# First expert's first unit as plain block products in two halves of 256 tokens, with the first loads issued from two engines

## The chip, the cores and the metric

The kernel runs on one core of a Trainium2 chip, in one launch. The metric is device time in microseconds (us), the median of the runs of a kernel.

## The reference

Two stages follow each other. The first is attention by chunks of 32 tokens (4 batches, 8 heads, 768 tokens, 64 dimensions), where each chunk sees 16 tokens to its left, 8 to its right and 8 memory keys per head:

```python
scores = scale * np.matmul(q_c, k_full.transpose(0, 1, 3, 2))
scores = scores - np.max(scores, axis=-1, keepdims=True)
a = np.exp(scores)
a = a / (np.sum(a, axis=-1, keepdims=True) + 1e-09)
out[:, :, c_start:c_end] = np.matmul(a, v_full)
```

Its output, as x of 3072 tokens by 512, goes through a layer of 8 experts (F = 1024), whose weights P come from exp of the logits by eight rounds of row and column normalisation:

```python
for e in range(E):
    h = np.maximum(x @ w1[e], 0.0)
    ye = h @ w2[e]
    out += P[:, e:e + 1] * ye
```

## The kernel before, in words

**Units.** The experts' work is cut into 48 units, each one expert and a group of 512 tokens (6 groups, 8 experts). A unit has four parts of the hidden dimension (`fp`, 0 to 3; tile names end in it). A unit's hidden products are px, py, pz (L1272), its output products yx, yy, yz or, for expert 0, yp (`plain_output`, L1684). The products have float32 accuracy: every operand is split into two fp16 parts under a power-of-two scale (`split`: the high part on ACT, L462, then the low part on VectorE, L470), and three products of the parts are added (`PASSES`). A group of operands has one scale; `scales` finds it from the largest magnitude: per-partition maxima on VectorE (`vmax` of v for x, L780; `mxs` of the weights, L503), a transposed row through PE (row_x, row_w, L443), the exponent on VectorE, and back to all partitions through PE (sp_x, sp_w, L430), then ux, sx (or uw, sw) at L405 and L406.

**Seven products.** Hidden products use a scheme of seven products over 2 x 2 blocks in place of eight; its operands are the blocks and four sums of blocks, made of x on GpSimd and VectorE (xt, L1019 to L1043) and of w1 on GpSimd (ws, L562, in `cut`), and split too. A unit takes 7 x 24 = 168 matmuls of 256 columns. Expert 0's outputs use w2 as it stands.

**Attention.** 24 blocks of 128 tokens, four to a group of x. For a block: `load_block`, `load_extra` and `load_values` issue its loads (v at L758 and memory values at L748, into a ring of two v tiles), `transposed` turns q and k (tq L817, tk L821, tx L695; copies qT, kC on ACT), `scores` makes sp on PE (L880), the maximum and the subtraction on VectorE (sm, s), exp on ACT (L924), the totals on VectorE, a product on GpSimd (s, L930), and `values` turns s (ta, L953), multiplies by v (xp, L963) and copies to xg. `build` makes the operands of a group of x; it needs all four blocks and their common scale. `logits` makes lp (L1089).

**First weights.** `first_weights` loads w1 and w2 of expert 0 through SP, takes the maxima and the scale, and calls `cut` for sums and splits.

**The order.** A planner in Python (`Plan`) takes tasks with an engine, a cost and a due time, and writes each engine's order by list scheduling. `START`, `TURN`, `UNIT`, `AHEAD` (50, 68, 36.7, 62) set the due times: `begin(n)` for unit n, `needed(n)` for block n of attention. Where it expects PE to be idle, `Plan.pad` puts warm matmuls (tile warm, L376), which compute nothing that is used. DMAs are issued by SP, and 16 by ACT (memory values of the first two blocks); an issue stands in the engine's order, and what comes behind it on that engine waits for it. Both engines' DMAs complete on one set of semaphores.

Of the kernel before, what the change touches and what calls it, by code (L numbers as in the profile page):

```python
# [203 lines left out]
def tile_chunked_attn_sinkhorn_moe(  # L204
# [28 lines left out]
    P = 128  # L233
# [58 lines left out]
    sx = misc.tile([P, NU], F32, name="sx")  # L292
    ux = misc.tile([P, NU], F32, name="ux")
    sw = misc.tile([P, E, 2], F32, name="sw")
    uw = misc.tile([P, E, 2], F32, name="uw")
    most_of = misc.tile([P, 2, NU + 2 * E + 1], F32, name="most_of")
# [12 lines left out]
    START, TURN, UNIT, AHEAD = 50.0, 68.0, 36.7, 62.0  # L309
# [229 lines left out]
    def cut(e, fp, which, st, ld, prio):  # L539
        s = sw[:, e, which - 1 : which]  # L540
        if e == 0 and which == 2:

            o = operands("w2", [P, 2, 7, DH], f"w2_{e}_{fp}")
            wide = "p a d -> p (a d)"
            done = split(
                lambda j: o.t[:, j, 0:4].rearrange(wide),
                lambda: st.t.rearrange(wide),
                s,
                [known[e, 2], ld],
                prio,  # L550
                (1.15, 1.28),
                [st, o],
            )
            wo[e, fp, 2] = (o, [done])
            return
# [31 lines left out]
        o = operands("w1" if which == 1 else "w2", shape, f"w{which}_{e}_{fp}")  # L587
# [14 lines left out]
        else:  # L602
# [9 lines left out]
        done = [split(d, src, s, deps, prio - 2, costs, [st, o]) for d, src, costs in parts]  # L612
        done.append(
            split(
                lambda j: o.t[:, j, 3:7].rearrange(flat),
                lambda: ws.t.rearrange(flat),
                s,
                deps + sums,
                prio,
                (1.15, 1.28),  # L620
                [ws, o],
            )
        )
        wo[e, fp, which] = (o, done)
# [11 lines left out]
    lgs = []  # L636

    BU = UT // QB
# [91 lines left out]
    def load_values(n):  # L730
# [8 lines left out]
        slot = n % 2  # L739
        vt = rings["v"].take(lambda k: v_tiles[k], slot)  # L740

        queue, eng = (nc.scalar, "ACT") if n < 2 else (nc.sync, "SP")

        def go_m():
            for par in range(2):
                p0 = par * KW + WIN
                for c in range(CB):
                    queue.dma_start(  # L748
                        vt.t[p0 : p0 + NM, c], mem_v[b, par::2].rearrange("h m d -> m h d")
                    )  # L750

        def go_v():
            for par in range(2):
                p0 = par * KW

                def part(c, r, t, m):

                    nc.sync.dma_start(  # L758
                        vt.t[p0 + r : p0 + r + m, c],
                        v[b, par::2, t : t + m].rearrange("h t d -> t h d"),  # L760
                    )
# [11 lines left out]
        at = needed(n) - 22.0  # L773
        lv = [add("SP", 2 * CB + 2 * (first or last), go_v, (), at, [vt], dma=2.5)]
# [13 lines left out]
        vfound.append(add("DVE", 1.21, most, lv, needed(n) - 3.0, [vt]))  # L788
        if n % BU == BU - 1:
            u = n // BU  # L790
            sxs[u] = scales(
                lambda: vmax[:, n + 1 - BU : n + 1],
                sx[:, u : u + 1],
                ux[:, u : u + 1],
                f"x_{u}",
                vfound[n + 1 - BU : n + 1],
                needed(n) - 2.0,
                "att",
            )
# [60 lines left out]
    def scores(n):  # L860
# [51 lines left out]
        t = add("PE", 1.5, go, made, at, [qT, kC, s], takes=sp)  # L912
# [72 lines left out]
    def build(u, at):  # L985
# [5 lines left out]

        def plain(i, kt, g, r):
# [12 lines left out]
        def sums(kt):  # L1005
# [53 lines left out]

        for kt in range(2):  # L1060
            plain(0, kt, g1, kt)
            sums(kt)
# [3 lines left out]
        xkept[u] = add(  # L1066
            "SP",
            1,
            lambda: nc.sync.dma_start(xkeep[u], x.t.rearrange("p a o k n -> p (a o k n)")),
            done,  # L1070
            at + 10.0,
            [x],
            dma=7.0,
        )
# [167 lines left out]
    def expert_scale(e, prio):  # L1242
        pscales[e] = add(
            "DVE",
            0.29,
            lambda: nc.vector.tensor_scalar(
# [6 lines left out]
            ),  # L1253
# [36 lines left out]
    def hidden(e, u, fp, hs, use_at, aside):  # L1290
# [5 lines left out]
        def run(dst, op, more, deps, takes=None):  # L1296
# [4 lines left out]
                    (w.t[:, wl, a, kt], x.t[:, xl, b, kt]) for kt in range(2) for wl, xl in PASSES  # L1301
# [365 lines left out]

    def plain_output(n, t, hs):

        e, u = units[n]  # L1670
# [4 lines left out]
        a = buf("acc", apool, [P, DM], F32, f"acc_{e}_{T}")  # L1675
        py = bank("main", [P, DM], f"yp_{e}_{T}")

        def part(fp):
            def go():
                hf, wf = hs[fp][0], wo[e, fp, 2][0]  # L1680
                for i, (fh, (hl, wl)) in enumerate(
# [5 lines left out]
                        wf.t[:, wl, 2 * fh : 2 * fh + 2].rearrange("p a d -> p (a d)"),  # L1687
# [7 lines left out]
        for fp in range(FP):  # L1695
# [4 lines left out]
                [t, *hs[fp][1], *wo[e, fp, 2][1]],  # L1700
                now[0],
                [hs[fp][0], wo[e, fp, 2][0]],
# [24 lines left out]
    def first_weights():  # L1727
        for which, at in ((1, START), (2, outputs_at(0) - 20.0)):
            found, staged = [], []
            for fp in range(FP):  # L1730
# [126 lines left out]
```

## Time and profile before

| What | us |
|---|---|
| median of 3 runs (1969.32 to 1970.98) | 1970.33 |
| the profiled execution | 1967.24 |
| its span | 1965.5 |
| PE busy | 1931.7 |
| VectorE (DVE) busy | 1465.9 |
| ScalarE (ACT) busy | 1031.5 |
| GpSimd (POOL) busy | 557.3 |

The profile is of one execution; the busy times add up rows that may overlap with other engines' work, and what an engine waits for is inferred from semaphores. Times in the tables and timelines count from the start of the span.

### The profile page before, as it was taken

What the parts mean: (1) busy time and instruction counts of PE and PEld (TensorE: products, weight loads), DVE (VectorE), ACT (ScalarE), POOL (GpSimd) and SP (SyncE); (2) the same over time, 40 slices, a digit from 0 to 9 for tenths busy, and PEclk for the clock granted to TensorE, in tenths of its full rate; (3) what the DMA queues carried; (4) which work ended last, traced back from release to release, by engine and by line L of the source; (5) the groups of instructions that cost most, each with busy time, mean ns of one, the idle gap of its engine ahead of it and who ended that gap; (6) DMA issues with size and microseconds to landing.
All of it is one profiled execution on the core that took longest, in us unless ns stands there. A gap on an engine that the chain in (4) does not pass through costs nothing.

```text
span 1965.5 us, 47252 instructions
## 1 busy us (share of the span) xinstructions
PE 1931.7 (98%) x19536; PEld 1665.8 (85%) x19536; DVE 1465.9 (75%) x2406; ACT 1031.5 (52%) x2014; POOL 557.3 (28%) x568
## 2 busy tenths in 40 slices
PE   8899999989999999999999999999999999999998
PEld 7776777768888888888888888888888888888887
DVE  4975655897678885798678886798678886787574
ACT  4655555555565564565455464565455464464353
POOL 2321111254214332342214322332214322232112
PEclk9999999999999999999999999999999999999999
DMA  7785532244413632343423642343423642322321
GB/s 163 177 236 148 134 95 71 103 156 145 143 74 103 218 137 89 111 156 135 137 79 97 220 140 82 118 157 128 141 81 98 208 152 81 108 82 82 124 82 65
DMA packets 242183, 248.45 MB, mean 126 GB/s; under 512 B 114736, under 2 KB 176176, under 8 KB 237616
## 3 DMA queue, kind: packets, MB, share of 16 engines
q1 hardware_dynamic: 241328, 245.31, 39.3%
q8 instruction: 153, 2.51, 0.5%
q14 instruction: 62, 0.51, 0.1%
q10 hardware_dynamic: 640, 0.13, 0.0%
HBM read 184.04 MB, written 61.34 MB: 125 GB/s over the span
## 4 chain that ended last, share of the span: by engine, by line
PE 92%; DVE 6%; DMA 1%; issue 0%; SPq 0%; ACT 0%; POOL 0%; ACTq 0%; DVEq 0%; POOLq 0%
PE px L1272 24%; PE yx L1272 22%; PE pz L1272 12%; PE yz L1272 11%; PE py L1272 6%; PE yy L1272 6%; PE yp L1684 6%; PE xp L963 2%; DVE ss L1428 1%; DVE c L1329 1%; DVE w L470 1%; PE sp L880 1%; DVE x L470 1%; PE ta L953 1%; DVE h L1472 1%; PE warm L376 1%
## 5 line engine op out<-in xcount | busy, mean ns | idle before, releaser
L1272 PEld LDWEIGHTS <-w 128*128 128x128 f16 x8064 | 788.3, 98 | 110.9 <-issue 16.7
L1272 PEld LDWEIGHTS <-h 128*128 128x128 f16 x7056 | 691.1, 98 | 82.7 <-ACT h L1439 1.0
L1272 PE MATMUL px<-x,w 128*128 128x256 f16 x4608 | 563.3, 273 | 12.1 <-DVE c L1329 12.0
L1593 POOL TENSOR_TENSOR acc<-acc,y 128x256 f32<-128x256 f32 x252 | 275.5, 1100 | 886.7 <-ACT y L1568 883.7
L1272 PE MATMUL yx<-w,h 128*128 128x256 f16 x4032 | 469.6, 273 | 1.4 <-ACT h L1439 0.7
L1319 ACT ACTIVATE q<-px 128x256 f32<-128x256 f32 x384 | 145.9, 381 | 317.5 <-PE px L1272 312.9
L1272 PE MATMUL pz<-x,w 128*128 128x256 f16 x2304 | 284.0, 273 | 2.3 <-ACT q L1319 2.3
L1272 PE MATMUL yz<-w,h 128*128 128x256 f16 x2016 | 233.8, 273 | 0.0
L1488 DVE TENSOR_TENSOR h<-ss,h 128x1024 f16<-128x1024 f32 x160 | 205.8, 1298 | 3.5 <-ACT h L1464 3.5
L1439 ACT ACTIVATE h<-c 128x768 f16<-128x768 f32 x168 | 140.8, 838 | 113.2 <-DVE c L1329 113.2
L1464 ACT CAST h<-ss 128x1024 f16<-128x1024 f32 x168 | 174.1, 1039 | 15.7 <-DVE ss L1428 15.7
L1472 DVE SCALAR_TENSOR_TENSOR h<-c,h 128x768 f16<-128x768 f32 x168 | 168.3, 1005 | 11.7 <-ACT h L1439 11.6
L1428 DVE SCALAR_TENSOR_TENSOR ss<-c,ss 128x256 f32<-128x256 f32 x336 | 166.8, 496 | 8.0
L1329 DVE SCALAR_TENSOR_TENSOR c<-px,q 128x256 f32<-128x256 f32 x192 | 78.2, 421 | 115.1 <-PE px L1272 111.3
L1272 PE MATMUL py<-x,w 128*128 128x256 f16 x1152 | 142.5, 273 | 0.0
L1568 ACT ACTIVATE y<-yx,pscale 128x256 f32<-128x256 f32 x168 | 79.3, 473 | 113.1 <-PE yx L1272 109.5
L1428 DVE SCALAR_TENSOR_TENSOR ss<-c,h 128x512 f32<-128x512 f32 x168 | 129.7, 772 | 7.5 <-ACT h L1416 6.3
L1684 PE MATMUL yp<-w,h 128*128 128x512 f16 x576 | 132.0, 379 | 0.0
L1329 DVE SCALAR_TENSOR_TENSOR c<-py,q 128x256 f32<-128x256 f32 x192 | 80.8, 424 | 68.2 <-PE py L1272 59.8
L1272 PE MATMUL yy<-w,h 128*128 128x256 f16 x1008 | 116.9, 273 | 0.0
L1684 PEld LDWEIGHTS <-h 128*128 128x128 f16 x576 | 55.2, 98 | 58.8 <-issue 0.8
L462 ACT ACTIVATE w<-ws,sw 128x1024 f16<-128x1024 f32 x60 | 68.5, 1142 | 64.9 <-POOL ws L562 64.9
(129 smaller groups left out, 1815.0 us busy)
## 6 DMA issues: line engine op xcount, KB each, us to landing
x<-xkeep SPq DMA_DIRECT2D x28, 1792.0 KB
akeep<-acc SPq DMA_DIRECT2D x168, 256.0 KB
acc<-akeep SPq DMA_DIRECT2D x168, 256.0 KB
w1f<-in_moe_w_dram SPq DMA_DIRECT2D x64, 256.0 KB
w2f<-in_moe_w_dram SPq DMA_DIRECT2D x32, 512.0 KB
w1fm<-in_moe_w_dram SPq DMA_DIRECT2D x56, 256.0 KB
w2fm<-in_moe_w_dram SPq DMA_DIRECT2D x28, 512.0 KB
xkeep<-x SPq DMA_DIRECT2D x6, 1792.0 KB
```

What stands on the lines that cost most here:

```text
L462: lambda: nc.scalar.activation(dst(0), src(), AF.Copy, scale=s),
L1272: nc.tensor.matmul(dst.t, a, b, start=(not more and n == 0), stop=(n == end), skip_group_check=more,)
L1319: lambda: nc.scalar.activation(t.t, src.t, AF.Copy, scale=DOWN),
L1329: lambda: nc.vector.scalar_tensor_tensor(c.t[:, o], src.t, DOWN, q.t, op0=ALU.mult, op1=ALU.add),
L1428: lambda: nc.vector.scalar_tensor_tensor(dst(), src(), 0.0, other(), op0=ALU.max, op1=op),
L1439: lambda: nc.scalar.activation(h.t[:, 0, 0:3], c.t, AF.Relu),
L1464: lambda: nc.scalar.copy(h.t[:, 0, 3:7], ss.t),
L1472: lambda: nc.vector.scalar_tensor_tensor(h.t[:, 1, 0:3].rearrange("p a n -> p (a n)"), c.t.rearrange("p a n -> p (a n)"), 0.0, h.t[:, 0, 0 ...
L1488: lambda: spare.tensor_tensor(h.t[:, 1, 3:7], ss.t, h.t[:, 0, 3:7], op=ALU.subtract),
L1568: (lambda: nc.scalar.activation(t.t, src.t, AF.Copy, scale=f))
L1593: lambda: nc.gpsimd.tensor_tensor(acc.t[:, cols], acc.t[:, cols], q.t, op=ALU.add),
L1684: nc.tensor.matmul(py.t, hf.t[:, hl, where[fh], o : o + P], wf.t[:, wl, 2 * fh : 2 * fh + 2].rearrange("p a d -> p (a d)"), start=(fp == 0 ...
```

## The change

The first unit (expert 0, tokens 0 to 511) computes its hidden products as eight plain block products per part, 192 matmuls of 256 columns (tile pp, L1830 of the changed kernel), in two halves of 256 tokens. The first half needs blocks 0 and 1 of attention alone and has a scale of its own (column NU of sx and ux); `expert_scale` corrects `pscale` for its tokens. w1 and w2 of expert 0 are split as they stand, 1024 columns at once. w1 is loaded a second time after that unit, for the sums of the later units, and the other operands of the group of x are made after it (`rest`). v of the first four blocks has four places, two of them in tiles of w2; the split x of block 2 and 3 lies partly in such a tile too. v of these blocks and w1, w2 of expert 0 are issued by SP and ACT in turn; memory values are loaded once per block and parity and copied twice by SP (`copy_m`) in place of eight loads. The planner's numbers change with it.

```diff
-    START, TURN, UNIT, AHEAD = 50.0, 68.0, 36.7, 62.0
+    START, TURN, UNIT, AHEAD = 44.0, 64.0, 36.7, 58.0
+    PACE = 46.0
...
+        if e > 0:
+            pieces = [(slice(3, 7), slice(0, 4), (1.15, 1.28))]
+        else:
+            pieces = [(slice(2, 3), slice(0, 1), (0.5, 0.65)), (slice(4, 7), slice(1, 4), (0.9, 1.1))]
+            deps = deps + o.users
...
+    def plain1(fp, st, ld, prio):
+        o = operands("w1", [P, 2, 7, 2, P], f"w1_0_{fp}")
+        done = split(
+            lambda j: o.t[:, j, 0:4].rearrange("p o k f -> p (o k f)"),
+            lambda: st.t.rearrange("p a k f -> p (a k f)"),
+            sw[:, 0, 0:1],
+            [known[0, 1], ld],
...
         if n < BU:
-            return 12.0 + 9.0 * n
-        return START + ((n + 1) / BU - 1.0) * AHEAD - 12.0
+            return 11.0 + 6.5 * n
+        return PACE + ((n + 1) / BU - 1.0) * AHEAD - 12.0
...
-        slot = n % 2
-        vt = rings["v"].take(lambda k: v_tiles[k], slot)
-        queue, eng = (nc.scalar, "ACT") if n < 2 else (nc.sync, "SP")
+        slot = n if n < BU else n % 2
+        if slot < 2:
+            vt = rings["v"].take(lambda k: v_tiles[k], slot)
+        else:
+            vt = rings["v"].take(
+                lambda k: room(k, 0, WIDE * 2)
...
+        if n < BU:
+            lv = [
+                add(eng, parts, lambda i=i, on=on: go_v((i,), on), (), at, [vt], dma=1.25)
+                for i, (eng, on) in enumerate((("SP", nc.sync), ("ACT", nc.scalar)))
+            ]
+        else:
+            lv = [add("SP", 2 * parts, lambda: go_v((0, 1), nc.sync), (), at, [vt], dma=2.5)]
         if vmem.get(slot) != b:
             vmem[slot] = b
-            lv.append(add(eng, 2 * CB, go_m, (), at + 0.1, [vt], dma=0.4))
+            eng, queue = ("ACT", nc.scalar) if n < BU else ("SP", nc.sync)
+            lv.append(add(eng, 2, go_m, (), at - 0.1, [vt], dma=0.1))
+            lv.append(add("SP", 2, copy_m, [lv[-1]], at + 0.1, [vt], dma=0.3))
...
+            (NU, n == BU // 2 - 1, START - 12.0),
...
-        t = add("PE", 1.5, go, made, at, [qT, kC, s], takes=sp)
+        t = add("PE", 0.9, go, made, at, [qT, kC, s], takes=sp)
...
+        if u == 0:
+            for i, (g, cs, k) in enumerate(
+                ((g1, c1, 0), (g1, c1, 1), (g2, c2, 1), (g2, c2, 0))
+            ):
...
+                v = NU if i < 2 else u
...
+                        cs + [sxs[v]],
...
+            def rest(at):
+                before = list(x.users)
...
+                for kt in range(2):
+                    sums(kt, at, done)
+                keep(at, done)
...
+            if e == 0:
+                nc.vector.tensor_scalar(
+                    pscale[:, 0, 0:TH],
...
+    def first_hidden(fp, g, h):
...
+        for i, fh in enumerate(((0, 1), (1, 0))[g]):
+            px = bank("main", [P, GT], f"pp_{nm}_{fh}")
+            t = None
+            for k in range(2):
+                def go(fh=fh, k=k, px=px):
+                    for n, (kt, (wl, xl)) in enumerate(
+                        (kt, p) for kt in range(2) for p in PASSES
+                    ):
+                        nc.tensor.matmul(
+                            px.t,
+                            w.t[:, wl, 2 * fh + k, kt],
+                            tokens(k, kt, xl),
...
+    def first_unit():
+        hs = [operands("h", [P, 2, 7, GT], f"h_0_{fp}") for fp in range(FP)]
+        for g in range(2):
+            made = [first_hidden(fp, g, hs[fp]) for fp in range(FP)]
+            for t in range(TH):
+                plain_output(0, g * TH + t, made)
...
-    first_weights()
+    def fetch_first(which, at, step):
+        found, staged = [], []
+        for fp in range(FP):
+            st, ld = load(0, fp, which, at - 42.0 + step * fp, eng=("SP", "ACT")[fp % 2])
...
+        if n == 0:
+            for fp, s in enumerate(fetch_first(2, START + 14.0, 2.0)):
+                plain2(fp, *s, START + 8.0 + 2.0 * fp, vs[fp][0].users if fp > 1 else [])
+            first_unit()
+            later[0](needed(BU + 1))
+            for fp in range(FP):
+                weights(0, fp, 1, begin(1) - 10.0 + 2.0 * fp)
+            maxima(1, begin(3))
+            continue
```

The order of PE ahead of the first hidden product, before (tq, tk and sp_1089 are the transposes and scores of block 5, lq a transpose of the logits):

```order
L430 MATMUL sp_x_969<-most_of,one 128x1
...
L817 MATMUL tq_980<-ident,q_680 128x128 x4
...
L1110 MATMUL lq_997<-ident,lt_972 128x128
L821 MATMUL tk_1003<-ident,k_682 128x128 x4
...
L880 MATMUL sp_1089<-kC,qT_989 32x64 x32
...
L1272 MATMUL px_0_0_1129<-x_999,w_0_0_759 128x256
```

The same place in the change (sp_611, ta and xp are of block 2, tk and sp_841 of block 3, tx of the second four blocks, x_657 holds the first half of x):

```order
L952 MATMUL sp_611<-kC,qT_539 32x64 x32
...
L445 MATMUL row_w_0_705<-ident,most_of 1x128
...
L1025 MATMUL ta_715<-ident,s_663 128x128 x4
L432 MATMUL sp_w_0_721<-most_of,one 128x1
...
L893 MATMUL tk_750<-ident,k_414 128x128 x4
L737 MATMUL tx_759<-ident,kx_408 128x128 x4
...
L1830 MATMUL pp_0_0_0_767<-x_657,w_0_0_727 128x256
...
L1035 MATMUL xp_800<-at_723,w_0_2_267 64x32 x32
L952 MATMUL sp_841<-kC,qT_741 32x64 x32
```

The first product moves from behind the scores of block 5 to a place ahead of the values product of block 2. Ahead of the first yp now stand 132 pp (of 192), ahead of the first px before stood the four values products that now lie among them in part; the change has 159 warm matmuls ahead of the first product (195 before) and 4 behind it.

ACT from its start to the first exp, before:

```order
L748 DMA v_144<-in_mem_v_dram 8x4x64 x8
L748 DMA v_145<-in_mem_v_dram 8x4x64 x8
L845 ACT_TABLE_LOAD
L845 ACTIVATE qT_233<-tq_228 128x512
...
L699 COPY kxT_273<-tx_268 128x512
...
L845 ACTIVATE qT_345<-tq_338 128x512
L924 ACTIVATE s_343<-s_343 128x512
```

and in the change:

```order
L796 DMA v_145<-in_mem_v_dram 8x4x64 x2
L815 DMA v_145<-in_v_dram 56x4x64 x4
L917 ACT_TABLE_LOAD
L917 ACTIVATE qT_213<-tq_208 128x512
L496 DMA w1f_1_228<-in_moe_w_dram 128x4x128 x2
...
L496 DMA w1f_3_241<-in_moe_w_dram 128x4x128 x2
L796 DMA w_0_2_267<-in_mem_v_dram 8x4x64 x2
...
L815 DMA w_0_2_267<-in_v_dram 56x4x64 x4
...
L815 DMA w_0_3_346<-in_v_dram 56x4x64 x4
L996 ACTIVATE s_349<-s_349 128x512
```

Ahead of the table load stand 13 issues (16 before); 16 more stand between the copies of block 0, the last ten behind kxT, and the first exp and block 1's qT come behind them.

VectorE ahead of the first output product, in the change (behind the second half of x):

```order
L472 SCALAR_TENSOR_TENSOR x_657<-xt_0_1169,sx,x_657 128x4x256
L407 TENSOR_SCALAR uw<-sp_w_0_1382 128x1
L408 RECIPROCAL sw<-uw 128x1
L963 MEMSET sp_1303 32x2x4x16
L966 TENSOR_REDUCE sm_1405<-sp_1303 128x2x4
L972 TENSOR_TENSOR s_1420<-sp_1303,sm_1405 128x2x4x64
L472 SCALAR_TENSOR_TENSOR w_0_0_1174<-w2f_0_764,sw,w_0_0_1174 128x1024
```

The first yp stands behind that last split, as before; ahead of it now stand also the low parts of four hidden tiles (512 columns each), sums of x and two splits of them, which before lay ahead of the first hidden product.

## Rows read from the trace of the kernel before

**Rows 1.** The page: its first line, section 1 and the chain by engine

```profile
span 1965.5 us, 47252 instructions
...
PE 1931.7 (98%) x19536; PEld 1665.8 (85%) x19536; DVE 1465.9 (75%) x2406; ACT 1031.5 (52%) x2014; POOL 557.3 (28%) x568
...
PE 92%; DVE 6%; DMA 1%; issue 0%; SPq 0%; ACT 0%; POOL 0%; ACTq 0%; DVEq 0%; POOLq 0%
```

**Rows 2.** PE by stretches: stretch, length, busy (instructions), granted clock, DMA share, GB/s

```profile
50.00:63.29 13.29, 8.52 (x138) 0.99 0.71 139
...
63.29:80.00 16.71, 16.71 (x187) 0.90 0.89 265
```

**Rows 3.** The same table for the warm tile alone, on PE

```profile
0.00:63.29 63.29, 27.52 (x195) 0.94 0.74 159
...
92.53:352.00 259.47, 2.46 (x18) 1.00 0.53 142
```

**Rows 4.** Timeline of PE, 0 to 64 us: start, duration, instruction, idle before

```profile
16.82 1.09 PE L817 MATMUL tq<-ident,q 128*128 128x128 f32 x4 [3.38 <-DMA q<-in_q_dram]
...
21.68 1.04 PE L880 MATMUL sp<-kC,qT 64*32 64x64 f32 x64
...
29.09 2.06 PE L963 MATMUL xp<-at,v 64*64 64x32 f32 x64
...
38.36 0.27 PE L443 MATMUL row_w<-ident,most_of 128*1 128x128 f32 x1
...
62.45 0.91 PE L880 MATMUL sp<-kC,qT 64*32 64x64 f32 x64 [4.37 <-DVE s L900]
...
63.29 2.74 PE L1272 MATMUL px<-x,w 128*128 128x256 f16 x12
```

**Rows 5.** Timeline of PE behind the first product

```profile
72.63 1.47 PE L1272 MATMUL px<-x,w 128*128 128x256 f16 x12
...
73.94 1.47 PE L1272 MATMUL pz<-x,w 128*128 128x256 f16 x12
...
92.53 5.34 PE L1684 MATMUL yp<-w,h 128*128 128x512 f16 x24
```

**Rows 6.** Timeline of ACT, its first entry (q: issuing of DMAs)

```profile
0.72 7.20 ACTq L748 DMA_DIRECT2D v<-in_mem_v_dram  x16
```

**Rows 7.** Tile w1f and tile v, 0 to 50 us, the issuing rows of SP

```profile
L494 SPq DMA_DIRECT2D w1f<-in_moe_w_dram x8: 497/511/1985, 19.7 to 29.1; - x8
...
L758 SPq DMA_DIRECT2D v<-in_v_dram x34: 288/412/1842, 7.4 to 44.6; - x34
```

**Rows 8.** All engines by stretches of 5 us: the columns of Rows 2, every engine's busy time

```profile
15.00:20.00 5.00, 3.18 (x15) 2.76 (x16) 2.17 (x4) 1.25 (x3) 0.00 (x0) 0.53 0.50 108
...
20.00:25.00 5.00, 4.98 (x116) 3.82 (x115) 2.81 (x5) 2.64 (x6) 1.04 (x1) 0.79 1.12 262
```

**Rows 9.** DVE by line and shape, 0 to 130 us: busy us, mean ns, idle before

```profile
L780 DVE TENSOR_REDUCE vmax<-v 128x1 f32<-128x1024 f32 x10 | 12.1, 1212 | 15.4 <-DMA v<-in_v_dram 15.4
...
L900 DVE TENSOR_TENSOR s<-sp,sm 128x512 f32<-128x512 f32 x9 | 6.2, 688 | 0.2
...
L894 DVE TENSOR_REDUCE sm<-sp 128x8 f32<-128x512 f32 x9 | 6.2, 686 | 1.7 <-PE sp L880 1.6
...
L908 DVE TENSOR_REDUCE sm<-s 128x8 f32<-128x512 f32 x9 | 6.1, 678 | 5.0 <-ACT s L924 5.0
```

**Rows 10.** Timeline of DVE, 40 to 91 us

```profile
40.31 0.16 DVE L406 RECIPROCAL sw<-uw 128x1 f32<-128x1 f32 x1
...
50.13 0.46 DVE L470 SCALAR_TENSOR_TENSOR w<-w1f,sw,w 128x256 f16<-128x256 f32 x1
...
54.27 0.94 DVE L470 SCALAR_TENSOR_TENSOR x<-xg,sx,x 128x256 f16<-128x256 f32 x1
...
90.99 5.00 DVE L470 SCALAR_TENSOR_TENSOR w<-w2f,sw,w 128x1024 f16<-128x1024 f32 x4
```

**Rows 11.** DVE by stretches

```profile
63.29:91.00 27.71, 26.07 (x48) 0.94 0.71 198
```

More of the change, by code (lines that the diff above doesn't have):

```diff
@@ L586, in cut @@
             shape = [P, 2, 7, DH]
-        o = operands("w1" if which == 1 else "w2", shape, f"w{which}_{e}_{fp}")
+        if e > 0:
+            o = operands("w1" if which == 1 else "w2", shape, f"w{which}_{e}_{fp}")
+        else:
+            o = wo[e, fp, which][0]
         sums = []
@@ L611, in cut @@
             flat = "p o d -> p (o d)"
[L612 to L621, printed above, removed]
-            )
-        )
-        wo[e, fp, which] = (o, done)
+        if e > 0:
+            done = [split(d, src, s, deps, prio - 2, costs, [st, o]) for d, src, costs in parts]
+        else:
+            done = wo[e, fp, which][1]
@@ new lines, in cut @@
+        if e > 0:
+            pieces = [(slice(3, 7), slice(0, 4), (1.15, 1.28))]
+        else:
+            pieces = [(slice(2, 3), slice(0, 1), (0.5, 0.65)), (slice(4, 7), slice(1, 4), (0.9, 1.1))]
+            deps = deps + o.users
+        for to, of, costs in pieces:
+            done.append(
+                split(
+                    lambda j, to=to: o.t[:, j, to].rearrange(flat),
+                    lambda of=of: ws.t[:, of].rearrange(flat),
+                    s,
+                    deps + sums,
+                    prio,
+                    costs,
+                    [ws, o],
+                )
+            )
@@ new lines, in cut, with room @@
+        wo[e, fp, which] = (o, done)
+    first2 = []
+    def room(fp, a, b):
+        return first2[fp].t.rearrange("p a o d -> p (a o d)")[:, a:b]
+    WIDE = 2 * DM
+    THIRD = 2 * WIDE
+    def plain1(fp, st, ld, prio):
[5 more added lines that the diff above has]
+            [known[0, 1], ld],
+            prio,
+            (1.15, 1.28),
+            [st, o],
+        )
+        wo[0, fp, 1] = (o, [done])
@@ L626, in weights, with block1, plain2 @@
+    def block1(e, i):
+        return i if e > 0 else (0, 1, 3, 2, 4, 5, 6)[i]
+    def plain2(fp, st, ld, prio, before):
+        done = split(
+            lambda j: room(fp, WIDE * j, WIDE * (j + 1)),
+            lambda: st.t.rearrange("p a d -> p (a d)"),
+            sw[:, 0, 1:2],
+            [known[0, 2], ld, *before],
+            prio,
+            (1.15, 1.28),
+            [st, first2[fp]],
+        )
+        wo[0, fp, 2] = (first2[fp], [done])
     def weights(e, fp, which, prio):
@@ L786, in most @@
             )
[L788 to L799, printed above, removed]
+        at = needed(n) - 3.0 if n >= BU else START - 14.0 + n // 2 * 17.0
+        vfound.append(add("DVE", 1.21, most, lv, at, [vt]))
+        for u, of, at in (
+            (n // BU, n % BU == BU - 1, needed(n) - 2.0 if n >= BU else START + 5.0),
+            (NU, n == BU // 2 - 1, START - 12.0),
+        ):
+            if of:
+                m = n % BU + 1
+                sxs[u] = scales(
+                    lambda m=m: vmax[:, n + 1 - m : n + 1],
+                    sx[:, u : u + 1],
+                    ux[:, u : u + 1],
+                    f"x_{u}",
+                    vfound[n + 1 - m : n + 1],
+                    at,
+                    "att",
+                )
         vs[n] = (vt, lv)
```

223 lines of the change are left out of this document (163 added, 60 removed).

## The prediction

> **What bounds the kernel now.** The page first: TensorE (PE) is busy 98% of the span and carries 92% of the chain that ended last [rows 1]. A time can therefore change in two ways only: by matmul work put in or taken out, and by PE time that is idle or filled with the warm matmuls (L376), which compute nothing. The table of PE by stretches says where the second kind lies: of the 13.29 us ahead of the first product PE is busy 8.52, and in the 16.71 us behind it all the time [rows 2]. The same table for the warm tile: 27.52 us of its busy time lie ahead of the first product, 2.46 between 92.53 and 352 us [rows 3]. The timeline of PE shows the order: scores of block 1 at 21.68, its values product at 29.09, scores of block 5 at 62.45 after 4.37 us of waiting for VectorE (DVE), first hidden product at 63.29 [rows 4]. So the first product waits for DVE, which is building the first unit's operands, and the start of the kernel is the place that the change works on. Steady state is untouched: apart from the end of the first expert the order of PE is the same there.
>
> How far can an earlier first product count? The first output product stands at 92.53 [rows 5], and from there on the rows of PE have few holes. I therefore measure both kernels at the first output product (yp): what is gained up to there, less the matmul work that is then still left over, is what the end gains.
>
> **Step 1, the opening loads.** Before, ACT issues 16 DMAs in 7.20 us, 0.45 each [rows 6]; PE then waits 3.38 us for q of block 1 [rows 4]. In the change ACT has 13 ahead of its table load and 16 more between its copies up to the first exp, 29 in place of 16 ahead of that exp. 13 more by 0.45 are 5.9 us, of which the 3.38 us of waiting can hide a part: block 1's scores move from 21.7 to between 24.2 and 27.6 if nothing else helps, and stay at 21.7 if the issues fit into ACT's waits. I take 25.0, near the lower of the two slips, since ACT is waiting for PE in much of that time. The upper bound is an issue that is held up: the longest loads of v and of w1 on SP took 1.84 and 1.99 us, against medians of 0.41 and 0.51 [rows 7].
>
> In return SP has half of the loads of v and of w1. The DMA engines have room for them early (share 0.50 from 15 to 20 us) and none from 20 to 25 us, where it is 1.12 at 262 GB/s with SP alone issuing [rows 8]. That row speaks for little gain from the second issuer. The Trainium skill, "DMA: Bandwidth & Descriptors", section "Issuing engines are not separate DMA queues", says the same as a rule: DMAs of all engines run on the same 16 DMA engines, and a second issuer saves only sequencer time. By the rule the loads would land no earlier where the share is full. The sum below doesn't need them earlier: all it wants is that they land before DVE asks.
>
> **Step 2, up to the first product.** From block 1's scores to the end of its values product it is 9.5 us before (21.68 to 29.09 + 2.06) [rows 4]. The change needs only blocks 0 and 1 there. Behind that come sp_x with its two scalars 0.6, block 2's maximum and subtraction 1.4 (2 x 0.69), the last maximum of w1 1.2, block 2's total 1.1 (0.68 and two small rows) [rows 9], the scale of w1 (from row_w at 38.36 to sw at 40.47 it was 2.1 before [rows 4, 10]; with a split of x of 0.75 between, 2.9), and the first split of w1, ACT's half 1.1 and DVE's 1.3. That is 19.1 us, so the first product stands at 25.0 + 19.1 = **44**, against 63.29. Bounds: 41 (scores of block 1 at 21.7) and 47 (at 27.6).
>
> **Step 3, from there to the first output product.** PE has 132 of the plain products of 256 columns ahead of yp. Two groups of 12 follow each other in 1.31 us [rows 5], so 0.109 each and 14.4 us; four values products of 2.06 are 8.2, four score products of 0.91 are 3.6 [rows 4]; transposes and logits make some 7 more: 33 us. DVE has, from the end of the first split of w1 to that of the first split of w2: four vmax and four maxima of w2, 8 x 1.21 = 9.7; four score pairs 5.5; three totals 3.2 [rows 9]; six splits 1024 wide, 6 x 1.28 = 7.7 (four took 5.00 [rows 10], and single ones up to 1.3); four hidden low parts and two x splits 512 wide, six of about 0.75, taken between the 0.46 of a free 256-wide one and 1.25 [rows 10]; three sums of x, 2.7; small scalars 2.5: 35.8 us. DVE is longer than PE, so it bounds this stretch, and PE will wait there a few us. Splits beside a busy GpSimd (POOL) are slower: 0.94 for a shape that takes 0.46 alone [rows 10]. For the x sums and splits of this stretch I add 1.7; small gaps and the overlapping ends of rows I let cancel. 37.5 us, so yp starts at 44 + 37.5 = **81.5** against 92.53: 11.0 us earlier. Bounds 36.1 (no slowing) and 41 (below).
>
> **Step 4, what is owed then.** A plain unit costs 192 products where the seven-product scheme takes 168. 60 of the 192 stand behind the first yp: 60 x 0.109 = 6.55 us; one transpose more is already done, so 6.1 us are owed. Of the 24 extra products alone the price would be 2.6 us; the rest is moved work.
>
> **Step 5, small ones.** Warm matmuls behind yp: 2.46 us before [rows 3], none in the change. If the waits that they fill vanish, that is a gain of 2.46; if PE just waits there, nothing. I take half, 1.2. The second unit's operands come later against PE than before: PE has 8.1 us of work between the last values product and the unit's first product, DVE and ACT some 9.2 (the splits and sums of step 3 once more): a stall of 1.1. The second load of w1 (2 MB, eight DMAs), its sums on POOL and the second splits of x_0 have some 40 us to be done in; POOL is busy 28% of the span [rows 1]; nothing. If that cover fails, the second unit waits, up to 3 us. The correction of pscale is one small DVE row: nothing.
>
> **Sum:** -11.0 + 6.1 - 1.2 + 1.1 = **-5.0 us**. The profiled execution took 1967.24 us, its span 1965.5; it is 3.1 us below the median of the three runs, 1970.33. So 1962.2 for a like execution, and 1965.3 as a median. A measurement of this kernel can tell 0.2%, 3.9 us, from no change; -5.0 lies just beyond it. The point of no gain is yp at 86.5, so a first product at 49.
>
> **The rivals.** *A, as summed* (0.55): 1965.3, with 1962 to 1968 by the bounds of steps 2 and 3.
>
> *B, more than that* (0.13): ACT's issues fit into its waits, block 1's scores stay at 21.7, the first product comes at 40.8, DVE's stretch takes its 36.1, and all 2.46 us of warm time go. yp at 77: -15.5 + 6.1 - 2.5 = -11.9, 1958.4. For it: ACT waits 3.38 us with PE for q_1 anyway. Against it: the splits beside POOL were slow in the only row that shows them.
>
> *C, no change* (0.20): DVE's stretch stretches. The 0.94 against 0.46 holds for every row with two operands in SBUF that meets POOL, and gaps of 6% (in the stretch of DVE behind the first product the busy time is 26.07 of 27.71 us [rows 11]) come on top: 41 in place of 37.5, yp at 85, -7.5 + 6.1 - 1.2 + 1.1 = -1.5, 1968.8. The Trainium skill, "SBUF — State Buffer", section "SBUF: two separate sides", has the rule behind the 0.94: a DVE operation with two SBUF inputs and a GpSimd operation lock each other out for the whole instruction. The row agrees (0.94 is 0.46 and the wait for about half a POOL row); by that rule C would be the likelier the more of POOL's sums fall beside these rows.
>
> *D, slower* (0.08): ACT's issues are held up. All DMAs of SP and ACT share a set of semaphores, so an issue of ACT can have to wait for a landing of SP's, and exp_0 is queued behind ten such issues. At the 1.84 to 1.99 us of the longest rows [rows 7] these ten take 19 us in place of 4.5; block 1's scores come at 39, the first product at 58, yp at 95.5: +3.0 + 6.1 - 1.2 + 1.1 = +9.0, 1979. It decides from a first product at 49 on. For it: the share of 1.12 at just that time [rows 8]; against it: the medians.
>
> *E, the second issuer does nothing* (within A): the scale of w1 stays where it was, sw at 40.47 [rows 10]; the first product then comes at 42.9 or later, no other than A.
>
> The last 0.04 are slips elsewhere, above all where expert 0 ends and the order of units differs.
>
> **How the numbers follow.** Forecast 1965.3. Range 1959.5 to 1972.0: A and C whole, the near part of B, and the small slips of 3 us on C; left out are the far part of B and D. Faster by over 0.2% (under 1966.4): most of A (0.45) and B, 0.58. Within: the rest of A and C, 0.30. Slower (over 1974.3): D and the slips, 0.12.
>
> **What would show it.** First plain product at 41 to 47; block 1's scores at 24 to 28, with ACT issuing ahead of the first exp; DVE busy without a hole of over 1 us between first product and yp; yp at 80 to 84; no stall over 2 us ahead of the second unit. Wrong would make it: issues of ACT over 1 us each, a w1 maximum waiting for its load, a PE stall behind yp for the second w1, or yp after 86.5.

## The result and the profile after

The changed kernel took 1971.22 us, the median of 22 runs (1967.47 to 1975.32). Beside it the kernel before took 1967.94 in 22 runs, its first three among them, whose 1970.33 lay high in that spread. The ratio is 1.0016, with a 95% interval of 1.001 to 1.0023: slower, by some 3.3 us, where 5.0 us less had been forecast. That is inside the 0.2% that the prediction took for no change, and inside its range; the direction was wrong.

The page of the changed kernel, its first line and busy times, against [rows 1]. This execution took 1972.38 us.

```profile
span 1970.6 us, 47172 instructions
...
PE 1929.7 (98%) x19511; PEld 1665.0 (84%) x19511; DVE 1465.3 (74%) x2405; ACT 1036.8 (53%) x2018; POOL 551.3 (28%) x568
```

The span is 5.1 us longer, while PE is busy 2.0 us less: time was lost to waiting. The timeline of PE shows where, from the scores of block 1 to the second unit's first product (start, duration, instruction, idle before and what ended it):

```profile
25.68 1.25 PE L952 MATMUL sp<-kC,qT 64*32 64x64 f32 x64 [3.59 <-ACT kC L897]
...
29.06 3.63 PE L1035 MATMUL xp<-at,v 64*64 64x32 f32 x64
...
36.56 2.06 PE L1035 MATMUL xp<-at,v 64*64 64x32 f32 x64
...
48.61 2.27 PE L1830 MATMUL pp<-x,w 128*128 128x256 f16 x18
...
58.53 0.86 PE L952 MATMUL sp<-kC,qT 64*32 64x64 f32 x64
...
65.48 1.09 PE L889 MATMUL tq<-ident,q 128*128 128x128 f32 x4 [6.09 <-DMA q<-in_q_dram]
...
91.84 6.64 PE L1909 MATMUL yp<-w,h 128*128 128x512 f16 x30
...
129.39 1.47 PE L1408 MATMUL px<-x,w 128*128 128x256 f16 x12
```

The last place in the kernel before:

```profile
122.19 1.47 PE L1272 MATMUL px<-x,w 128*128 128x256 f16 x12
```

Against [rows 4, 5]: the scores of block 1 come at 25.68 (21.68 before), the first hidden product (pp) at 48.61 in place of 63.29, and then PE stands for 6.09 us, waiting for q of block 5. The first output product (yp) comes at 91.84, 0.7 us earlier than before, and the second unit's px at 129.39, where it was at 122.19 before.

PE by stretches (stretch, length, busy, instructions in brackets, granted clock, DMA share, GB/s), the two places where it lost most:

```profile
20.00:25.00 5.00, 1.61 (x13) 0.98 0.60 128
25.00:30.00 5.00, 4.30 (x91) 0.50 1.23 264
30.00:35.00 5.00, 5.00 (x63) 0.50 0.63 121
60.00:65.00 5.00, 0.00 (x0) 0.74 0.56 123
65.00:70.00 5.00, 4.52 (x25) 0.58 1.08 271
...
48.61:91.84 43.23, 36.08 (x733) 0.92 0.56 128
91.84:129.39 37.55, 37.55 (x474) 1.00 0.82 227
```

From 25 to 35 us the granted clock is 0.50, the lower of the two levels, 1.2 GHz; before that PE had been busy only 1.61 of 5 us from 20 to 25. From 60 to 65 PE did nothing, and from 65 to 70 the granted clock is 0.58: the hole costs its 6.09 us, and time at the lower clock behind it. From the first output product to the second unit's first product PE is never idle.

What was q of block 5 waiting for? SP issues it. The timeline of SP (an entry is a run of issues):

```profile
46.12 14.02 SPq L815 DMA_DIRECT2D v<-in_v_dram  x10
60.51 1.46 SPq L804 DMA_DIRECT2D w<-w  x2
62.07 0.39 SPq L764 DMA_DIRECT2D q<-in_q_dram  x1
```

Ten loads of v of block 5 take 14.02 us, then come two copies, then q at 62.07. The table of SP's waits from 40 to 66 us (line, what it waited for, us, times, longest) names one wait that matters, and the timeline of ACT has the loads of w2 that it means (its first row is from the opening, four loads of v):

```profile
SPq L815 <- DMA w2f<-in_moe_w_dram: 8.7, 1, 8.7
...
15.48 4.12 ACTq L815 DMA_DIRECT2D w<-in_v_dram  x4
...
51.25 0.40 ACTq L498 DMA_DIRECT2D w2f<-in_moe_w_dram  x1
...
54.99 0.40 ACTq L498 DMA_DIRECT2D w2f<-in_moe_w_dram  x1
```

SP waits 8.7 us for w2, which ACT loads and no load of v has any use for. The two engines' DMAs complete on one set of semaphores. In this program's order, a DMA is issued when the one before it on its semaphore has landed, whichever engine issued that. The waits that the program gives to ACT's load of w2 (part 1) and to SP's fourth load of v of block 5:

```
L498 DMA w2f_0_1_836<-in_moe_w2_dram 128x2x512 [waits DMAHW3_49,DVE_49]
L815 DMA v_1_145<-in_v_dram 48x4x64 [waits DMAHW3_49,PE_49]
```

Both have DMAHW3. ACT's load also waits for VectorE, since it goes into the staging buffer of a part of w1, which VectorE has to have split first. The timeline of VectorE:

```profile
49.95 1.28 DVE L472 SCALAR_TENSOR_TENSOR w<-w1f,sw,w 128x1024 f16<-128x1024 f32 x1
...
61.50 1.22 DVE L847 TENSOR_REDUCE vmax<-v 128x1 f32<-128x1024 f32 x1 [5.44 <-DMA v<-in_v_dram]
```

That split ends at 51.23, and ACT issues w2 at 51.25; by the trace's semaphore events it lands at 56.6, and SP's fourth load follows. Of the wait of 8.7 us some 3.3 lie ahead of ACT's issue, and 5.3 are w2's own transfer. So a load of v on SP hung on a split on VectorE and then on the landing of w2, by way of a semaphore, with no data in common. Queued behind it on SP were six more loads of v, two copies and q of block 5; VectorE's maximum of v waited 5.44 us with PE.

### The profile page after: what moved, and what is told of

The parts are those of the page before. It is cut to its first block, busy times and chain, and to the rows that moved or that the text cites. A ratio compares the mean times of both kernels' runs of the same rounds, so it can differ in the third digit from the quotient of the medians.

```text
span 1970.6 us, 47172 instructions
## 1 busy us (share of the span) xinstructions
PE 1929.7 (98%) x19511; PEld 1665.0 (84%) x19511; DVE 1465.3 (74%) x2405; ACT 1036.8 (53%) x2018; POOL 551.3 (28%) x568
## 4 chain that ended last, share of the span: by engine, by line
PE 86%; DVE 6%; issue 0%; ACT 0%; DVEq 0%; ACTq 0%
PE px L1408 23%; PE yx L1408 22%; PE pz L1408 11%; PE yz L1408 11%; PE py L1408 6%; PE yy L1408 6%; PE yp L1909 4%; DVE ss L1566 2%; PE xp L1035 2%; DVE c L1467 1%; DVE w L472 1%; DVE h L1610 1%; PE sp L952 1%; PE ta L1025 0%; PE tk L893 0%
## 5 line engine op out<-in xcount | busy, mean ns | idle before, releaser
L1408 PEld LDWEIGHTS <-w 128*128 128x128 f16 x7896 | 772.1, 98 | 110.7 <-issue 15.3
L1408 PEld LDWEIGHTS <-h 128*128 128x128 f16 x7056 | 690.2, 98 | 82.8 <-ACT h L1577 1.0
L1408 PE MATMUL px<-x,w 128*128 128x256 f16 x4512 | 551.7, 273 | 14.7 <-DVE c L1467 11.2
L1408 PE MATMUL pz<-x,w 128*128 128x256 f16 x2256 | 277.7, 273 | 1.0 <-ACT q L1457 1.0
L464 ACT ACTIVATE w<-ws,sw 128x1024 f16<-128x1024 f32 (+1 forms) x64 | 69.4, 1090 | 62.7 <-POOL ws L549 62.7
```

The source lines that it names most:

```text
L464: lambda: nc.scalar.activation(dst(0), src(), AF.Copy, scale=s),
L1408: nc.tensor.matmul(dst.t, a, b, start=(not more and n == 0), stop=(n == end), skip_group_check=more,)
```

## The experiments

All times below are medians, of 22 runs for the changed kernel, five and six for the two kernels made from the one before, and eleven for the others; the ratio is to the kernel before, run beside them on the same chip. Runs 1 to 4, 5 to 8 and 9 to 11 were on three different chips, where the kernel before took 1967.41, 1966.45 and 1967.29, so times of different groups are compared by their ratios. The places are from each kernel's timeline of PE: scores of block 1, first hidden product, first output product, second unit's first product.

| Kernel | scores 1 | first product | first yp | second unit | time | ratio (95%) |
|---|---|---|---|---|---|---|
| before | 21.68 | 63.29 | 92.53 | 122.19 | | 1 |
| changed | 25.68 | 48.61 | 91.84 | 129.39 | 1971.22 | 1.0016 (1.001 to 1.0023) |
| 1: w2 from SP | 25.98 | 48.40 | 82.79 | 121.05 | 1964.15 | 0.9981 (0.9972 to 0.999) |
| 2: w1 and w2 from SP | 23.13 | 44.43 | 82.33 | 119.88 | 1965.26 | 0.9988 (0.9979 to 0.9996) |
| 3: v from SP | 24.14 | 44.38 | 88.82 | 126.47 | 1970.09 | 1.0014 (1.0005 to 1.0023) |
| 4: all from SP | 22.96 | 43.58 | 85.57 | 123.30 | 1966.0 | 0.9987 (0.9978 to 0.9996) |
| 5: w2 from POOL (GpSimd) | 25.30 | 49.09 | 87.48 | 125.02 | 1965.66 | 0.9994 (0.9985 to 1.0003) |
| 6: as 1, more warm matmuls | 26.06 | 45.74 | 82.35 | 120.51 | 1962.55 | 0.998 (0.9971 to 0.9989) |
| 7: as 1, v of blocks 2, 3 from SP | 22.46 | 43.76 | 84.38 | 121.92 | 1965.6 | 0.9995 (0.9986 to 1.0004) |
| 8: before, two issuers | 20.13 | 68.68 | 105.09 | 134.76 | 1978.9 | 1.0066 (1.0054 to 1.0079) |
| 9: as 1, rest of x_0 later | 26.08 | 49.70 | 83.95 | 122.55 | 1965.16 | 0.999 (0.9981 to 0.9998) |
| 10: as 6, rest of x_0 later | 26.23 | 45.91 | 81.00 | 120.64 | 1964.11 | 0.9983 (0.9974 to 0.9992) |
| 11: as 8, w2 from SP | 20.24 | 69.16 | 97.97 | 127.63 | 1972.75 | 1.003 (1.0019 to 1.0042) |

### 1: w2 from SP

```diff
-        queue = nc.scalar if eng == "ACT" else nc.sync
+        queue = nc.scalar if eng == "ACT" and which == 1 else nc.sync
```

> The changed kernel, with the two loads of w2 (expert 0, parts 1 and 3) that ACT issued now issued by SP; the order of PE, DVE and POOL is the same, ACT's differs by these two issues. Theory (the two issuers are tied together by the shared completion semaphores: SP's loads of v for block 5 wait for ACT's load of w2, which itself waits for a split of w1): the 8.7 us wait of SP on w2 and the 6.09 us hole of PE ahead of the transposes of block 5 (59.4 to 65.5) are gone or under 1 us, the first output product moves from 91.8 to about 86, and the time falls by 4 to 6 us, to 1965 to 1967. Rival (the hole is SP's own work and the traffic, v for blocks 4 and 5 being 18 loads in a row): the hole stays within 1 us of 6, and the time within 1.5 us of the changed kernel's.

PE by its timeline and SP by its own, at the place of the hole:

```profile
59.11 0.66 PE L889 MATMUL tq<-ident,q 128*128 128x128 f32 x4
...
82.79 6.64 PE L1909 MATMUL yp<-w,h 128*128 128x512 f16 x30
...
121.05 1.47 PE L1408 MATMUL px<-x,w 128*128 128x256 f16 x12
...
45.95 5.24 SPq L815 DMA_DIRECT2D v<-in_v_dram  x10
...
52.79 0.39 SPq L764 DMA_DIRECT2D q<-in_q_dram  x1
```

The ten loads of v take 5.24 in place of 14.02 us, q of block 5 goes out at 52.79, and its transpose has no idle time ahead of it. The first output product comes 9.0 us earlier, more than expected and more than the hole. From the first product to there PE has 6.6 us less of idle time, and 2.2 us less of busy time for the same 733 instructions (33.88 against 36.08), with a granted clock of 1.00 in that stretch in place of 0.92. The time falls from 1.0016 to 0.9981 of the kernel before, by about 6.9 us. The order of PE, VectorE and POOL is that of the changed kernel. The theory holds, and the rival (SP's own work and the traffic) falls: the loads of v are the same and in the same order.

### 5: w2 from POOL

```diff
-        queue = nc.scalar if eng == "ACT" else nc.sync
+        queue = (nc.scalar if which == 1 else nc.gpsimd) if eng == "ACT" else nc.sync
```

> The changed kernel, with the two loads of w2 that ACT issued now issued by POOL, whose DMAs complete on semaphores other than those that SP and ACT share; they still wait for the same split of w1, so they start no earlier than the 51.25 and 54.99 of the changed kernel. Theory (SP was held by the shared semaphore, not by w2 being late nor by where w2's issue stood on ACT): the 6.09 us hole is under 1 us, SP has no wait on w2 over 1 us ahead of block 5's q, the first output product comes at 82 to 84, the time is 1963.5 to 1966. Rival (w2's transfer itself, 1 MB at that time, holds v and q up; with SP issuing, the gain came from w2 being sent later): the hole stays at 3 us or more, since w2 travels when it did.

The timeline of POOL with the two issues, that of PE at the place of the hole, SP's first issue of w2, and VectorE's longest wait behind 48 us:

```profile
52.02 1.02 POOL L498 DMA_DIRECT2D w2f<-in_moe_w_dram  x1 [6.56 <-DMA v<-in_v_dram]
55.53 0.73 POOL L498 DMA_DIRECT2D w2f<-in_moe_w_dram  x1 [2.48 <-DVE w L472]
...
59.85 0.66 PE L889 MATMUL tq<-ident,q 128*128 128x128 f32 x4
...
54.69 2.60 SPq L498 DMA_DIRECT2D w2f<-in_moe_w_dram  x1
...
65.48 1.22 DVE L505 TENSOR_REDUCE mxs<-w2f 128x1 f32<-128x1024 f32 x1 [3.36 <-DMA w2f<-in_moe_w_dram]
```

w2 leaves as late as in the changed kernel (52.02 and 55.53), but the hole is gone: what held SP was neither w2's traffic nor its being late, but the semaphore that they shared. What was missed is a new wait: VectorE stands for 3.36 us for w2, and the first output product comes at 87.48 instead of 82 to 84. The load that it waits for is not one of POOL's, which landed 5.6 and 7.9 us after their issues, at 57.7 and 63.5. By the trace's semaphore events it is SP's first load of w2, issued at 54.69 and landed at 65.45, 10.8 us later; in run 1 SP's first load of w2 took 5.7 us. That POOL's two loads, in flight beside it, made it late is likely, but not shown. The time, 1965.66, was inside what was expected.

### 8 and 11: the two issuers alone, on the kernel before

```diff
-        queue = nc.scalar if eng == "ACT" else nc.sync
+        queue = nc.scalar if e == 0 and not ahead and fp % 2 == 1 else nc.sync
...
-                    nc.sync.dma_start(
+                    (nc.scalar if n < 4 and par == 1 else nc.sync).dma_start(
```

> The kernel before, its order of PE unchanged, with the second part of the change alone: half of the loads of v of the first four blocks and of w1 and w2 of expert 0 issued by ACT, at the places in the program where SP issued them. Theory (a second issuer brings nothing by itself and ties the queues together): the first product comes no earlier than 62.5, and the time is 0 to 6 us above the kernel before. Rival (SP alone is the slow part of the opening): w1's scale is known 2 us or more ahead of 40.5, the first product comes 1 to 3 us earlier and the time falls with it.

SP's longest waits up to 90 us (L758 is a load of v, L722 one of q), ACT's loads of v in the opening, and PE's timeline:

```profile
SPq L758 <- DMA w2f<-in_moe_w_dram: 10.6, 2, 9.9
SPq L722 <- DMA w2f<-in_moe_w_dram: 8.3, 1, 8.3
...
25.40 5.13 ACTq L758 DMA_DIRECT2D v<-in_v_dram  x4
...
31.40 1.25 PE L880 MATMUL sp<-kC,qT 64*32 64x64 f32 x64 [4.16 <-ACT kC L825]
...
68.68 2.74 PE L1272 MATMUL px<-x,w 128*128 128x256 f16 x12
...
88.29 2.72 PE L1272 MATMUL py<-x,w 128*128 128x256 f16 x12 [4.01 <-DVE c L1329]
```

The second part of the change by itself costs 12.5 us, twice the most that was expected. SP again waits for ACT's w2, once 9.9 us ahead of a load of v and once 8.3 us ahead of q. In the opening four loads of v take ACT 5.13 us, PE waits 4.16 us for the copy behind them, and the scale of w1 is known at 47.01, not earlier than the 40.47 of [rows 10]: the rival falls. One thing does come earlier: the scores of block 1 (20.13 against 21.68), without the wait of 3.38 us for q. The Trainium skill, "DMA: Bandwidth & Descriptors", section "Issuing engines are not separate DMA queues", has it that a second issuer saves no more than sequencer time. Run 8 agrees in that w1's scale comes no earlier for it, and shows a cost that goes beyond that rule.

Run 11 takes w2 back to SP:

```diff
-        queue = nc.scalar if e == 0 and not ahead and fp % 2 == 1 else nc.sync
+        queue = nc.scalar if e == 0 and which == 1 and not ahead and fp % 2 == 1 else nc.sync
```

> The kernel of the eighth experiment (the kernel before with two issuers), with w2 issued by SP again, so that v and w1 alone are shared between the issuers. Theory (the tie through w2 was most of the 12.5 us): SP's wait of 9.9 us on w2 is gone, the wait of 4.0 us of PE on VectorE behind the first product too, and the time falls by 6 to 10 us, to 1 to 6 us above the kernel before. Rival (ACT's issues of v in the opening cost it): the time falls by less than 4 us.

The wait on w2 and PE's wait of 4.01 us behind the first product are gone, and 7.0 us of the 12.5 with them, as expected. The rest, 5.5 us over the kernel before that it ran beside, stays with ACT's issues of v and w1, the only edit that is left; PE still waits in the opening for ACT's copy, 4.35 us.

### 2, 3 and 4: which loads ACT issues

The edits send w1 as well, or v in place of the weights, or both from SP. In 2 and 4 the `queue` of expert 0's loads is `nc.sync`; in 3 and 4:

```diff
-                for i, (eng, on) in enumerate((("SP", nc.sync), ("ACT", nc.scalar)))
+                for i, (eng, on) in enumerate((("SP", nc.sync), ("ACT", nc.sync)))
```

> As the run before, and the four issues of w1 (parts 1 and 3) that ACT had are SP's too; v is still issued by both. Theory (an issue on ACT holds the copies and the exp behind it): block 1's scores come 1 to 3 us earlier than 25.7 and the first product with them; the time falls by that much below the run with w2 alone moved. Rival (SP is the fuller queue, so w1's loads land later and its scale is late): block 1's scores move by less than 1 us, the last maximum of w1 waits for its load, and the first product is no earlier than 48.6.

> The changed kernel with all loads of v issued by SP, w1 and w2 still by both. Theory (ACT's issues of v ahead of the first exp cost the opening): block 1's scores come at 21 to 23 us in place of 25.7, PE's clock does not fall to 0.50 from 25 to 35 us, and the first product comes at 44 to 46; the hole of 6 us behind it stays, so the time falls by 1 to 4 us. Rival (SP, with all of v, is later than ACT was): block 1's scores come at 25 or later and the time stays or grows.

> The changed kernel with v, w1 and w2 all issued by SP; ACT issues only the memory values. Theory (the second issuer costs more than it saves): both holes go, block 1's scores come at 21 to 23, the first product at 43 to 46, the first output product at 81 to 84, and the time is 8 to 10 us under the changed kernel's, 1961 to 1963. Rival (one issuer can't bring 29 more loads in time): block 1's scores at 26 or later, the first product at 49 or later, and the time no better than the run with w2 alone moved.

In all three block 1's scores come earlier (22.96 to 24.14 against 25.68), the granted clock from 25 to 35 us is 1.00, and the first product comes at 43.6 to 44.4. So ACT's issues of w1 and v did cost the opening 4 to 5 us; taking back either of them already brings 4. In run 3, with w2 still on ACT, PE's hole is 6.48 us and the ratio that of the changed kernel (1.0014 and 1.0016), where 1 to 4 us less had been expected: the tie through w2 is what decides. Run 2 had been expected to be faster than run 1 by 1 to 3 us, and is not. Run 4 missed what was expected of it, 1961 to 1963; with everything issued by SP, PE waits three times for q. The first of these waits is in the kernel before as well (3.38 us), the other two stand behind the first product:

```profile
18.96 1.09 PE L889 MATMUL tq<-ident,q 128*128 128x128 f32 x4 [3.56 <-DMA q<-in_q_dram]
...
51.31 0.63 PE L889 MATMUL tq<-ident,q 128*128 128x128 f32 x4 [2.76 <-DMA q<-in_q_dram]
...
59.25 0.82 PE L889 MATMUL tq<-ident,q 128*128 128x128 f32 x4 [1.70 <-DMA q<-in_q_dram]
```

What is won ahead of the first product is lost behind it: from there to the first output product it is 37.90 us in run 2 and 41.99 in run 4, against 34.39 in run 1. Runs 1, 2 and 4 cannot be told apart by their intervals.

### 6 and 7: the opening of run 1

```diff
-        for _ in range(n):
+        filled.append(n)
+        for _ in range(n + MORE.get(len(filled), 0)):
...
+    MORE = {4: 18, 7: 28}
```

> The first experiment's kernel (w2 from SP), with 18 more warm matmuls ahead of block 0's scores and 28 more ahead of block 1's, about 2.0 and 3.1 us of PE in the 2.24 and 3.31 us where PE waits for ACT there. Theory (those waits make PE's clock fall to 0.5 from 26 to 36 us, which costs 3.4 us between block 1's scores and the end of its values product): the clock stays at 1.0 from 25 to 35 us, the values product of block 0 takes 2.1 in place of 3.6 us, the first product comes 2 to 4 us earlier than 48.4; of it 1 to 3 us reach the first output product (82.8) and the time (1964.15), which VectorE may bound. Rival (VectorE and the loads of w1 set the first product): the clock stays up, but the first product is within 1 us of 48.4 and the time within 1 us of 1964.15.

PE's timeline and its stretches (columns as above):

```profile
26.06 0.93 PE L955 MATMUL sp<-kC,qT 64*32 64x64 f32 x64 [0.64 <-ACT kC L900]
...
28.66 2.06 PE L1038 MATMUL xp<-at,v 64*64 64x32 f32 x64
...
45.74 2.27 PE L1833 MATMUL pp<-x,w 128*128 128x256 f16 x18
...
82.35 6.64 PE L1912 MATMUL yp<-w,h 128*128 128x512 f16 x30
...
25.00:30.00 5.00, 3.89 (x123) 1.00 1.15 266
30.00:35.00 5.00, 4.87 (x92) 1.00 1.24 184
```

With warm matmuls in the two waits the granted clock stays at 1.00 from 25 to 35 us (run 1 has 0.78 and 0.54), the values product of block 0 takes 2.06 in place of 3.63 us, and the first product comes 2.7 us earlier. That is what the slow clock cost. But the first output product moves by 0.4 us only, where 1 to 3 had been expected, and by its ratio the time cannot be told from run 1's: that half of the expectation fell to the rival. The other way to the same end:

```diff
-                for i, (eng, on) in enumerate((("SP", nc.sync), ("ACT", nc.scalar)))
+                for i, (eng, on) in enumerate((("SP", nc.sync), ("ACT", nc.scalar if n < 2 else nc.sync)))
```

> The first experiment's kernel (w2 from SP), with the loads of v of blocks 2 and 3 issued by SP alone, so that ACT has 10 issues fewer ahead of the first exp (8 of v; the four memory loads stay). Theory (ACT's issues behind kxT hold the first exp and block 1's qT): block 1's scores come at 22 to 24 in place of 26.0 and the first product at 44 to 46; the first output product 0 to 3 us earlier, the time 1962 to 1964. Rival (SP's queue gets longer and q and k of blocks 4 and 5 come late): a wait for q over 1 us appears in front of a transpose, and the time is 1964 to 1967.

Block 1's scores come at 22.46 and the first product at 43.76, and PE then waits 2.15 us for q of block 4; the first output product is later than in run 1, and no gain is left. Both sides of the expectation came true, in that order.

### 9 and 10: who bounds the stretch up to the first output product

```diff
                 before = list(x.users)
+                ready.extend(wo[0, fp, 2][1][0] for fp in range(FP))
```

> The first experiment's kernel (w2 from SP), with the sums of x_0 and their splits, which no early unit needs, made to wait for the splits of w2: 5 to 6 us of VectorE's rows move from ahead of the first output product to behind it. Theory (with w2 from SP the stretch from the first product at 48.4 to the first output product at 82.8 is PE's own, PE being busy in nearly all of it, not VectorE's as the prediction had it): the first output product stays within 1 us of 82.8 and the time within 1.5 us of 1964.15. Rival (VectorE bounds that stretch): the first output product comes at 78 to 80, and the time falls by 2 to 4 us.

> The sixth experiment's kernel (w2 from SP, more warm matmuls), with the same rows of x_0 moved behind the splits of w2. There the first product stood at 45.7 and the first output product at 82.35, 36.6 us with two holes of PE and a dip of its clock. Theory (with the earlier first product VectorE is the later one there): PE's holes ahead of the first output product shrink, it comes at 79 to 81, and the time falls by 1 to 3 us below 1962.55. Rival (PE's own work and its clock set it): the first output product stays at 82 and the time within 1 us.

In run 1 the two engines' busy times from first product to first output product (first PE, then VectorE):

```profile
48.40:82.79 34.39, 33.88 (x733) 1.00 0.70 160
...
48.40:82.79 34.39, 33.29 (x57) 1.00 0.70 160
```

The same for run 9:

```profile
49.70:83.95 34.25, 33.81 (x734) 1.00 0.70 161
...
49.70:83.95 34.25, 30.40 (x55) 1.00 0.70 161
```

In run 1 PE is busy 33.88 of 34.39 us and VectorE 33.29, so the busy times alone do not decide. Run 9 moves three sums and two splits, 4.7 us of rows, behind the splits of w2. VectorE's busy time in the stretch falls by 2.9 us only, since other rows take their place in part, and the stretch stays at 34.25: PE bounds it. The first product comes 1.3 us later in run 9, so the first output product, at 83.95, is just outside the 1 us that was expected. With the earlier first product of run 6, run 10 shortens the stretch from 36.6 to 35.1 us, so there VectorE had a part; but the time, 1964.11, shows none of it.

## Why the prediction was wrong, step by step

**What bounds it**, that the start decides and that the end follows the first output product: right. Measured by the timelines of before and after, the end moved by -0.7 (yp) + 7.9 (from yp to the second unit, 37.55 against 29.66) - 2.1 (from there to the end) = +5.1, the difference of the spans.

**Step 1** had block 1's scores at 25.0; they came at 25.68. The size was right, the sum was not, so that is in part luck: ACT has the 13 issues more, but not at 0.45 us each. The ten behind kxT take it from 15.48 to 23.85, 8.4 us in place of 4.5, and four of them 4.12.

**Step 2** had 19.1 us from there to the first product; it took 22.9. The missing term is PE's clock: the waits that step 1 foresaw let it fall to 0.50 for ten microseconds. With the clock held up (run 6) it took 19.7. The kernel before shows such a fall too: 0.53 from 15 to 20 us [rows 8], where PE waits 3.38 us for q [rows 4].

**Step 3 is where it failed.** It had 37.5 us to the first output product, VectorE's own work, and no wait on a load; it took 43.2. Its condition, "all it wants is that they land before DVE asks", did not hold, since SP was tied to ACT's load of w2. Without that tie the same order takes 34.4 us (run 1), and then neither VectorE's 37.5 nor its being the bound was right. Its rows in that stretch add up to 35.4 us (35.8 in the list), but it is busy for 33.3: I let their overlapping ends cancel against gaps that were not there, and added 1.7 for GpSimd, and PE's 33 us (33.88 measured) set the end. (The lower bound of 36.1 was 0.3 above what the list adds up to.) With w2 on SP, yp comes at 82.8, where 81.5 was forecast, and the kernel is 0.19% faster than the one before, 3.7 us by that ratio, where 5.0 was forecast. That this is near the forecast is luck in part: step 2 was 3.3 us too short for run 1 (22.4 against 19.1), step 3 3.1 us too long.

**Rival D** named the shared semaphores and priced one direction: ACT held by SP's landings. That happened, on a small scale: the four loads of v at 15.48 took over 1 us each, one of the signs of being wrong, and by the trace's semaphore events three of them went out within 0.02 us of the landing of a DMA of SP. The costly direction was the other: SP held by ACT's load of w2, which waits for VectorE. I listed what was queued behind ACT's issues, and did not ask what each of them waits for and which of SP's DMAs comes next on its semaphore. That could be read in the order beforehand.

**Steps 4 and 5**, +6.1 - 1.2 + 1.1 = +6.0: measured 7.9 - 2.1 = +5.8. The stall of 1.1 us ahead of the second unit did not come, PE being busy in all of the 37.55 us, so the parts fit less well than the sum. The reload of w1 costs nothing that shows.

**Rival B** (earlier still) had the first product at 40.8; the earliest in any run is 43.58, and it gained nothing by it. **Rival C** (1968.8) lay nearest to the measured time, by a mechanism that no run showed: VectorE's rows in that stretch add up to no more than listed (run 1).

## What to carry to other kernels

In this program two engines that issue DMAs on one set of semaphores are in part one queue: a load that waits for a buffer on the one stopped unrelated loads on the other. Before a load is moved to a second issuer, look what that load itself waits for, and which DMA follows it on its semaphore. The load into a reused buffer, w2, cost 6.9 us here (changed kernel against run 1). v and w1 on ACT were not free either: 4 to 5 us of the opening in the changed kernel, of which the time shows nothing, and 5.5 us of the time in the kernel before (run 11).

Of the versions tried, the changed kernel with w2 issued by SP alone (run 1, 0.9981, or 0.998 with more warm matmuls) is faster than both kernels, the one before and the changed one, by an interval that excludes 1; it is 0.2%. Its first product is not the earliest of the runs: those at 43.6 to 44.4 (runs 2, 4, 7) have ratios of 0.9987 to 0.9995, no better, and behind their first product PE waits for q (1.33 us in run 2, 2.76 and 1.70 in run 4, 2.15 in run 7).

## What the runs showed of the hardware

An idle PE paid twice: 3.59 us of waiting ahead of block 1's scores, in a stretch where it was busy 1.61 of 5 us, were followed by ten at half the clock, in which a values product took 3.63 us in place of 2.06. 46 warm matmuls in that wait and the one before it removed this (run 6, on run 1's order). The hole of 6.09 us was followed by a granted clock of 0.58 from 65 to 70 us. Issues that waited on a semaphore held ACT and the copies behind them: four loads of v took 4.12 us in the changed kernel and 5.13 in run 8. With w2 on POOL, SP had no such wait, POOL's loads landed 5.6 and 7.9 us after their issue, and SP's load of w2 beside them took 10.8 us (run 5).
